# A reordering of place 0's rest in a recurrence and mixture-of-experts kernel, with four more sums in exact parts

## The chip, the cores and the metric

The kernel runs on one core of a Trainium2 chip. The metric is device time in microseconds, as a median over runs. A core has five engines with queues of their own: TensorE (PE in the profile; its weight loads are shown as PEld), VectorE (DVE), ScalarE (ACT), GpSimd (POOL) and SyncE (SP), which here only issues transfers. TensorE writes to PSUM, 8 banks of 2 KB per partition; the other data lie in SBUF.

## The reference

A gated linear attention over 4 batches, 8 heads, 768 steps and a head size of 48, whose output rows (3072 of 384 numbers) go to a mixture of 8 experts, of which each row visits one.

```
for t in range(S):
    state = alpha[:, :, t, :, None] * state + np.einsum('bhd,bhe->bhde', k[:, :, t], v[:, :, t])
    y[:, :, t] = np.einsum('bhd,bhde->bhe', q[:, :, t], state)
x = y.transpose(0, 2, 1, 3).reshape(B * S, H * D)
logits = x @ w_gate
expert_idx = np.argmax(logits, axis=1)
gate_w = softmax(logits)[np.arange(N), expert_idx]
for e in range(E):
    rows = expert_idx == e
    out[rows] = gate_w[rows, None] * (np.maximum(x[rows] @ w1[e], 0.0) @ w2[e])
```

## The kernel before

**Attention.** The 768 steps are cut into 6 chunks of 128. With 4 batches that makes 24 units `s`; `s // 4` is the chunk, `s % 4` the batch. The loop `for i in range(-4, NT)` is a software pipeline written out by hand: iteration ("step") `i` does the scores of unit `i`, the transposes of unit `i + 1`, the operands of unit `i + 2`, the logits and stored rows of unit `i - 2`, and the running sums of the logarithms of alpha of a unit ahead. The order in which the code calls these functions is the order of each engine's queue (`manual_schedule`); only the waits between engines are found automatically.

- `load` (L388) puts the transfers of alpha, k, q and v on SP. `singly` and `loads_for` set which units are loaded in which step, one at a time at first, then in pairs.
- `logs` (L396) takes the logarithm of alpha on ACT. `cums` (L413) turns it into running sums by one float32 matmul of 128 x 384 and takes `exp` of it with both signs on ACT (L419, L420). For units from `APART` = 11 on, the logarithm is split: ACT writes a float16 part `hi` (L401), DVE the remainder `lo` (L406), and two matmuls (L415, L416) add up the two parts. `sums_to` says how many units' sums are done by step `i`: units 4 and 5 in step 1, 6 and 7 in step 2, 8 in step 3, and so on. The second sum of steps 0 to 2 comes after `attend`.
- `operands` (L462) multiplies k and q by these exponentials on POOL. `transposes` (L472) turns them on PE; DVE or ACT copies the result (L476, L478). `scores` (L485), `mask` (DVE, L493), `read_state` (L512), `attend` (L522), `keys_values` (L533) and `rows` (L559) are PE's work in a step.
- `scale_state` (L500, POOL) decays a unit's state. In the first unit of a chunk it needs `decay_cols` of that step (PE L453, DVE L455). In step 4 it stands ahead of the operands on POOL; in steps 8, 12, 16 and 20 behind them.

**Routing and early rows.** From step 5 on, DVE and POOL count, rank and place the rows by expert. The experts' "places" are processed one after another, largest capacity first. In step 21 the first 256 rows of place 0 (`EARLY`) are gathered (`early_gather`). In step 23 `early_turn` transposes them (L647) ahead of the masks, and `early_layer1` (L654) computes their hidden layer while the last units are routed.

**Place 0's rest.** After the attention, the 168 remaining rows of place 0 are computed. The order is: the gather of them (L822, POOL); layer 2 of early block 0 in two halves (`early_layer2`, L1181) and its scatter (L1046 on ACT, L1050 on POOL); the gather of place 1; the first half of early block 1; `turn` (PE L832, copies L833) of the rest; the second half of early block 1 and its scatter; `rest_layer1` (L1193), whose eight hidden tiles f0 to f7 are evicted in turn by ACT (even ones, L1201) and DVE (odd ones, L1198). Behind each odd one DVE does a piece of `places()` (L1125 to L1169), the bookkeeping for rows that do not fit. Then come the weights and the gather of place 2, POOL's copies of it (L842) for SP's transposing transfers (L843), DVE's weight sums for place 1, and `rest_layer2`: three sums of eight matmuls (L1209) with a copy each (L1212), between which `turn` of place 1 and DVE's `row_sums` are called.

**Places 1 to 7** use a scheme with seven products in place of eight (L938, L1003, L1020), which needs the sums of weights (L193, L196) and of rows that DVE prepares.

Of the kernel before, what the change touches and what calls it, by code (L numbers as in the profile page):

```python
# [8 lines left out]
F32 = mybir.dt.float32  # L9
# [11 lines left out]
def kernel(  # L21
# [43 lines left out]
    HC = C // 2  # L65


    APART, HS = 11, 512.0
    assert NB * C == S and FB * C == F and DB * C == Dm and D <= DP


# [1 line left out]
    SR = NJ * C  # L73
    CAP0, STEP = 424, 8
    caps = [CAP0 - STEP * i for i in range(E)]
    EARLY = 256
    CG = 2
    NG = NB // CG
    TG = CG * B
# [292 lines left out]
    with tc.tile_pool(name="ld", bufs=6) as ld, \  # L372
# [11 lines left out]
        def load(s, n, many):  # L384
# [6 lines left out]
            for i in range(many):  # L391
                st[s + i][n] = t[:, i]

        def logs(s):
            t = work.tile([C, Dm], F32, name="lna", bufs=4)
            nc.scalar.activation(t[:], st[s]["a"].rearrange("s h d -> s (h d)"), AF.Ln)  # L396
            st[s]["lna"] = t
            if s >= APART:

                st[s]["hi"] = work.tile([C, Dm], F16, name="hi", bufs=2)  # L400
                nc.scalar.mul(st[s]["hi"][:], t[:], HS)  # L401
# [7 lines left out]

        def cums(s, bank="cum"):  # L410
            cum = ps.tile([C, 512], F32, name="cum", tag=bank)
            if s < APART:
                nc.tensor.matmul(cum[:, :Dm], lhsT=cum_m[:], rhs=st[s]["lna"][:], start=True, stop=True)  # L413
            else:
                nc.tensor.matmul(cum[:, :Dm], lhsT=cum_h[:], rhs=st[s]["hi"][:], start=True, stop=False)  # L415
                nc.tensor.matmul(cum[:, :Dm], lhsT=cum_r[:], rhs=st[s]["lo"][:], start=False, stop=True)  # L416
            cp = work.tile([C, Dm], F32, name="cp", bufs=6)
            icp = work.tile([C, Dm], F32, name="icp", bufs=6)
            nc.scalar.activation(icp[:], cum[:, :Dm], AF.Exp, scale=-1.0)  # L419
            nc.scalar.activation(cp[:], cum[:, :Dm], AF.Exp)  # L420
            st[s]["cp"], st[s]["icp"] = cp, icp
# [42 lines left out]
                    d[e][:].rearrange("s (a p d) -> s a p d", a=2, p=NP), op=ALU.mult,  # L464
                )

        def transposes(s):
            d = st[s]
            for i, n in enumerate(("kT", "qT")):
                tp = ps.tile([C, NP, C], F32, name="tp", bufs=2)  # L470
                for p in range(NP):
                    nc.tensor.transpose(tp[:, p, :], pair(kqb[s % 3][:, i], p), ident[:])  # L472
                d[n] = work.tile([C, NP, C], F32, name=n)

                if 0 < s < B - 1 or i and s < NT - B - 2:
                    nc.vector.tensor_copy(d[n][:], tp[:])  # L476
                else:
                    nc.scalar.copy(d[n][:], tp[:])  # L478
# [124 lines left out]

        loaded = dict(a=0, k=0, q=0, v=0)

        singly = {-5: "aakq", -4: "kqav", -3: "akq", -2: "aav", -1: "kq", 0: "avakq", 1: "vkq"}

        def load_next(n, many):
            load(loaded[n], n, many)
# [28 lines left out]
        eg["h"] = early.tile([C, FB, EARLY], F32, name="h0")  # L638
        held = {}

        def early_turn():
            t = ld.tile([C, 2, H, D], F32, name="k_sb", bufs=3)
            eg["xT"] = t.rearrange("p b h d -> p (b h d)").rearrange("p (a t) -> p a t", a=DB)
            for j in range(EARLY // C):
                tp = ps.tile([C, DB, C], F32, name="tp", bufs=2)
                for a in range(DB):
                    nc.tensor.transpose(tp[:, a, :], eg["xg"][:, j, a * C : (a + 1) * C], ident[:])  # L647
                nc.scalar.copy(eg["xT"][:, :, j * C : (j + 1) * C], tp[:])

        def early_layer1(f):  # L650
            hp = ps.tile([C, NP, C], F32, name="tp", bufs=2) if f % 3 else ps.tile([C, NP, C], F32, name="sB")
# [44 lines left out]
        for i in range(-4, NT):  # L696
            loads_for(i)
            do(scores, i)
            if i < NT - 1:
                do(result, i - 1)  # L700
            do(logits, i - 2)
            if i >= B:
                do(add_state, i - 1)
            do(gate, i - 2)
            if i > 0:
                for s in new_logs(i):
                    logs(s)
            if i == NT - 1:
                early_turn()
            if 0 < i < NT and i % B == 0:  # L710
                decay_cols(i // B)
            do(mask, i, 0)
            do(mask, i, 1)
            if i < B:
                do(add_state, i - 1)
            do(transposes, i + 1)
            sums = list(new_sums(i))
            for s in sums[:1]:
                cums(s)
            if i < 0:  # L720
                for s in sums[1:]:
                    cums(s, "x")
            do(gate_weight, i - 2)
            route(i)
            for s in new_logs(i):
                if s >= APART:
                    low_part(s)
            do(keep_rows, i - 2)
            if len(sums) == 1:
                decay_out(sums[0])  # L730
            if i == -1:
                for s in range(2):
                    decay_out(s)

            if B - 1 <= i < 2 * B - 1:
                decay_out(i + 1, (1,))
            if i == NT - 2:
                si = next(se)[1]
                eg["si"] = lambda j, r: si[:r, j : j + 1]
            if i == B:  # L740
                scale_state(i)
            do(operands, i + 2)
            if i > B and i % B == 0:
                scale_state(i)
            if 0 < i + 1 < NT and (i + 1) % B == 0:
                decay_rows((i + 1) // B)
            elif i >= 0:
                do(scale_state, i + 1)
            one_hots(nc.gpsimd, *on_gpsimd.get(i, ()))
            do(read_state, i)  # L750
            do(attend, i)
            if i == NT - 2:
                result(i)
            if i >= 0 and sums[1:]:
                cums(sums[1])
                for s in sums:
                    decay_out(s, (0,) if i else (0, 1))
            do(keys_values, i)
            if i == NT - 3:
                held["tok"] = ps.tile([C, NC], F32, name="tok", tag="cum")  # L760
                tokens(held["tok"][:], *range((NG - 1) * TG))
                se = early_gather()
            do(rows, i - 1)
            if i in counts_in:
                counts(counts_in[i], counted(i - 1))
            if i < 0:
                for s in new_sums(i + 1):
                    logs(s)
            if i == -3:
                second_consts()  # L770
            if i in (-4, 0, 1):
                for j in {-4: (0, 1, 2), 0: (3,), 1: (4,)}[i]:
                    late_consts(j)
            if 12 <= i < 22:
                fetch_part(groups[0], i - 12)
# [397 lines left out]
    def cols_of(t, c0):  # L1173
        return lambda j, r: t[:r, c0 + j : c0 + j + 1]

    def early_layer2(j, part):

        if part == 0:
            eg["z"] = mps.tile([C, 512], F32, name="pA", tag="pA")
        for f in range(part * FH, (part + 1) * FH):  # L1180
            nc.tensor.matmul(  # L1181
                eg["z"][:, :Dm], lhsT=eg["h"][:, f, j * C : (j + 1) * C], rhs=groups[0]["w2"][:, f, :],
                start=(f == 0), stop=(f == FB - 1),
            )

    def rest_layer1(g, beside):
        n = g["n"]
# [27 lines left out]
    g0["gi"], g0["si"] = cols_of(g_e, EARLY // C), cols_of(s_e, EARLY // C)  # L1215

    gather(g0)
    early_layer2(0, 0)
    pl = places()
    early_layer2(0, 1)  # L1220
    scatter(eg, 0, C, eg["z"][:, :Dm])
    gp, sp = next(pl)
    for i, g in enumerate(groups[1:], 1):
        g["gi"], g["si"] = cols_of(gp, i * NJ), cols_of(sp, i * NJ)
    gather(groups[1])
    early_layer2(1, 0)
    for _ in turn(g0):
        pass
    early_layer2(1, 1)
    scatter(eg, 1, C, eg["z"][:, :Dm])  # L1230
    def beside(i):

        work = [z_halves(groups[i - 1])]
# [6 lines left out]
    for i, g in enumerate(groups):  # L1240
# [17 lines left out]
            layer1(g, beside(i), begin, last)  # L1258
        else:
            rest_layer1(g, pl)  # L1260
        if i == 0:
            weights(1, 2)
        weights(i + 2, 1)
        if i + 2 < E:
# [10 lines left out]

        def turned():
            if i == 0:
                yield from turn(nxt)
                row_sums(nxt)
                return  # L1280
            z_whole(groups[i - 1], nc.scalar.copy, 0, 1)
            yield
            if nxt:
                row_sums(nxt)
            z_whole(groups[i - 1], nc.scalar.copy, 2)
            z_whole(groups[i - 1], nc.vector.tensor_copy, 3)
            yield
            if i + 2 < E:
                for _ in x_halves(groups[i + 2]):
                    pass  # L1290
            yield
# [5 lines left out]
        if last:  # L1297
            for _ in between:
                pass
            for j, r in blocks(g):  # L1300
                rows_layer2(g, j, (*([] if j == 0 else ready), FH - 1, FB - 1))
                scatter(g, j, r, g["z"][:r, :Dm], shared=j == NJ - 2)
        elif i:
            rest[0](lambda: ahead(*((1,) if i == E - 2 else (1, 2))), between)
        else:
            ahead(1)
            rest_layer2(g, 0)
            next(between)
            rest_layer2(g, 1)
            next(between, None)  # L1310
            rest_layer2(g, 2)
        weights(i + 2, 2)
    in_order.close()
# [51 lines left out]
```

## Time and profile before

| what | value |
|---|---|
| median of 8 runs | 402.53 us (400.36 to 407.0) |
| the profiled execution's own time | 400.35 us |
| its span, first to last instruction | 398.6 us |
| mean granted TensorE clock | 0.995 |
| PE, PEld, DVE, ACT, POOL busy | 96, 82, 53, 56, 37% |
| HBM read, written | 49.00 MB, 9.58 MB |
| attention: first scores to last | 9.2 to 132 us |
| place 0's rest: first L1181 to first L938 | 148.3 to 181.2 us |

Times in the trace are microseconds from the span's start. A line of the timeline gives start, duration, engine, source line, operation, output and inputs, shape and count, and in brackets the idle time before it with what ended it. A float32 matmul appears as two records. Busy times of PE are no proof that it runs at its peak, since matmul ends are modelled; the distance between the starts of two groups is a better measure.

### The profile page before, as it was taken

The numbers are of one execution on the slowest core, as the hardware profiler recorded it, in microseconds if no ns is written. First come the engines' busy times: TensorE is split into PE (matmuls) and PEld (weight loads), VectorE is DVE, ScalarE is ACT, GpSimd is POOL, SyncE is SP. The second block draws the span as 40 slices with busy tenths as digits, with TensorE's granted clock in tenths as the row PEclk, the third lists the DMA queues.
The fourth block names the chain that finished last, engine by engine and source line by source line (L and its number), as shares of the span: only waits on it lengthen the run. The fifth ranks groups of instructions, "written<-read, shape, count | busy, mean of one in ns | idle before, by whom it ended". The sixth has DMA issues, their size and how long they took to land.

```text
span 398.6 us, 9107 instructions
## 1 busy us (share of the span) xinstructions
PE 384.4 (96%) x3390; PEld 327.3 (82%) x3390; DVE 212.9 (53%) x651; ACT 224.9 (56%) x515; POOL 148.5 (37%) x203
## 2 busy tenths in 40 slices
PE   7999999999999999879999999999999999999994
PEld 4678888888888875869979979979979979979852
DVE  5554656776666574374771682582483483561200
ACT  5575767777655430114466766765765766763640
POOL 6547464599587004850023016007007003011041
PEclk9999999999999999989999999999999999999999
DMA  9999998999964118689247768667866965611311
GB/s 172 193 215 225 203 228 182 227 207 243 242 189 139 64 41 296 216 228 215 42 181 175 163 184 186 197 199 168 213 197 158 218 197 130 188 23 53 59 57 55
DMA packets 153905, 67.44 MB, mean 169 GB/s; under 512 B 136699, under 2 KB 148082, under 8 KB 153860
## 3 DMA queue, kind: packets, MB, share of 16 engines
q1 hardware_dynamic: 148756, 57.13, 59.8%
q0 software_dynamic: 3408, 9.64, 8.0%
q8 instruction: 27, 0.44, 0.5%
q10 hardware_dynamic: 1696, 0.08, 0.3%
q14 instruction: 18, 0.15, 0.1%
HBM read 49.00 MB, written 9.58 MB: 147 GB/s over the span
## 4 chain that ended last, share of the span: by engine, by line
PE 66%; issue 22%; POOL 4%; DVE 2%; ACT 2%; DMA 2%; POOLq 0%; ACTq 0%; DVEq 0%
PE pA L938 7%; PE pC L1020 5%; PE sA L485 5%; PE tp L472 5%; PE y L522 5%; PE pB L938 5%; PE pA L1003 4%; PE x L559 4%; PE pA L1181 3%; PE y L512 3%; POOL out_dram L1050 3%; PE pC L938 2%; PE pB L1003 2%; PE tp L654 2%; PE cum L413 2%
## 5 line engine op out<-in xcount | busy, mean ns | idle before, releaser
L1050 POOL DMA_INDIRECT out_dram<-zo,sp x25 | 26.0, 1039 | 137.5 <-ACT zo L1075 127.4
L193 DVE TENSOR_TENSOR h_sb<-pB,u 128x208 f32<-128x208 f32 (+6 forms) x56 | 20.1, 359 | 53.5 <-PE pB L938 39.6
L462 POOL TENSOR_TENSOR kqb<-k_sb,icp 128x384 f32<-128x384 f32 x23 | 22.9, 998 | 31.4 <-PE y L533 18.1
L1020 PE MATMUL pC<-h_sb,w 128*128 128x416 f32 (+5 forms) x96 | 33.9, 496 | 0.0
L880 ACT COPY u<-pA 128x208 f32<-128x208 f32 (+6 forms) x68 | 21.2, 311 | 18.5 <-PE pA L1003 11.5
L938 PE MATMUL pA<-t,s 128*128 128x208 f32 (+6 forms) x112 | 28.6, 337 | 0.8
L485 PE MATMUL sA<-qT,kT 48*128 48x128 f32 x192 | 27.7, 284 | 0.9 <-DVE qT L476 0.9
L485 PE MATMUL sB<-qT,kT 48*128 48x128 f32 x192 | 27.7, 285 | 0.0
L938 PE MATMUL pA<-xgT,w 128*128 128x208 f32 (+6 forms) x112 | 27.7, 329 | 0.0
L822 POOL DMA_INDIRECT xg<-x_rows,gp x25 | 24.2, 967 | 7.0 <-issue 6.8
L472 PE MATMUL tp<-ident,kqb 128*128 128x128 f32 x192 | 26.2, 279 | 0.6 <-DVE kqb L462 0.6
L1020 PEld LDWEIGHTS pC<-h_sb,w 128*128 128x128 f32 x96 | 18.0, 190 | 10.3 <-issue 3.7
L485 PEld LDWEIGHTS sA<-qT,kT 48*128 48x128 f32 x192 | 23.1, 187 | 3.8 <-ACT kT L478 1.1
L949 ACT ACTIVATE h_sb<-h_sb 128x208 f32<-128x208 f32 (+6 forms) x28 | 10.3, 366 | 25.2 <-DVE h_sb L193 22.0
L938 PE MATMUL pB<-t,w 128*128 128x208 f32 (+6 forms) x112 | 23.8, 335 | 0.0
L462 POOL TENSOR_TENSOR kqb<-q_sb,cp 128x384 f32<-128x384 f32 x23 | 23.0, 1001 | 1.8 <-DMA q_sb<-in_q_dram 1.5
L541 ACT COPY yT<-y 128x512 f32<-128x512 f32 x24 | 14.0, 585 | 16.8 <-PE y L533 9.4
L472 PEld LDWEIGHTS tp<-ident,kqb 128*128 128x128 f32 x192 | 20.5, 140 | 3.4 <-issue 1.2
L938 PE MATMUL pC<-xgT,w 128*128 128x208 f32 (+6 forms) x112 | 23.1, 329 | 0.0
L485 PEld LDWEIGHTS sB<-qT,kT 48*128 48x128 f32 x192 | 23.1, 187 | 0.0
L493 DVE TENSOR_TENSOR dA<-sA,cmask 128x512 f32<-128x512 f32 x24 | 16.5, 688 | 10.7 <-PE sB L485 10.5
L938 PEld LDWEIGHTS pA<-t,s 128*128 128x128 f32 x112 | 19.1, 189 | 3.3 <-ACT u L880 2.0
(264 smaller groups left out, 991.0 us busy)
## 6 DMA issues: line engine op xcount, KB each, us to landing
w<-in_moe_w_dram SPq DMA_DIRECT2D x14, 1536.0 KB
x_rows<-xs SPq DMA_DIRECT2D x24, 192.0 KB
v_sb<-in_v_dram SPq DMA_DIRECT2D x10, 384.0 KB
k_sb<-in_k_dram SPq DMA_DIRECT2D x9, 384.0 KB
q_sb<-in_q_dram SPq DMA_DIRECT2D x9, 384.0 KB
a_sb<-in_alpha_dram SPq DMA_DIRECT2D x8, 384.0 KB
a_sb<-in_alpha_dram SPq DMA_DIRECT2D x8, 192.0 KB
w<-in_moe_w_dram SPq DMA_DIRECT2D x6, 256.0 KB
```

Of the source, the lines that this page charges most:

```text
L193: eng.tensor_tensor(out, a, b, op=ALU.add)
L462: eng.tensor_tensor(by_half(kq[:, i]), d[n].rearrange("s (a p) d -> s a p d", a=2), d[e][:].rearrange("s (a p d) -> s a p d", a=2, p=NP), ...
L472: nc.tensor.transpose(tp[:, p, :], pair(kqb[s % 3][:, i], p), ident[:])
L485: nc.tensor.matmul(t[:, p, :], lhsT=d["kT"][r : r + D, p, :], rhs=d["qT"][r : r + D, p, :], start=True, stop=True,)
L493: nc.vector.tensor_tensor(t[:], d["sc"][i][:], cmask[:, None, :].to_broadcast([C, NP, C]), op=ALU.mult)
L522: nc.tensor.matmul(yv(g)[o : o + D, j, :], lhsT=d["v"][:, g * NP + p, :], rhs=d["d" + "AB"[g]][:, p, :], start=(s < B and j == 0), stop=Tr ...
L822: nc.gpsimd.indirect_dma_start(out=g["xg"][:r, j, :], out_offset=None, in_=x_d[:, :], in_offset=bass.IndirectOffsetOnAxis(ap=g["gi"](j, r) ...
L880: nc.scalar.copy(t[:, :m], bank["A"][:, :m])
L938: nc.tensor.matmul(out, lhsT=ops[n_][0], rhs=ops[n_][1], start=first and n_ == names[0], stop=True, skip_group_check=True,)
L1003: nc.tensor.matmul(out, lhsT=lhs, rhs=rhs, start=first and f == 0, stop=True, skip_group_check=True)
L1020: nc.tensor.matmul(d2[:, :n], lhsT=w2[:, f, 2 * C :], rhs=h[:, f, :n], start=(f == 0), stop=(f == FB - 1),)
L1050: ins = nc.gpsimd.indirect_dma_start(out=out[:, :], out_offset=bass.IndirectOffsetOnAxis(ap=g["si"](j, r), axis=0), in_=zo[:r], in_offset= ...
```

## The change

It has five edits.

1. Sums in exact parts start at unit 9 instead of 11, and units 5 and 7 have them too. The `lo` of 5 and 7 is made on DVE inside `transposes`, between the copies of kT and qT.
2. Alpha 8 and 9 are loaded one at a time, alpha 8 ahead of v, k and q in step 1.
3. In step 8, as in step 4, `scale_state` stands ahead of the operands.
4. `early_turn` is split: block 0 is turned behind `read_state` of the last step, block 1 behind its `attend`.
5. Place 0's rest: the second half of early block 1 goes behind `rest_layer1`, in a PSUM buffer of the transposes (`tp`); its scatter goes with it, and so on POOL ahead of the gather of place 2. All of place 1's `turn` goes ahead of the weight sums and of the first `rest_layer2`, whose 24 matmuls follow one another; `row_sums` comes behind the first of the three.

`EARLY` is written as `2 * C`, which is 256 as before.

```diff
-    APART, HS = 11, 512.0
+    APART, HS = 9, 512.0
...
+        def apart(s):
+
+            return s >= APART or s in (5, 7)
...
-            if s >= APART:
+            if apart(s):
...
-            if s < APART:
+            if not apart(s):
...
-        def transposes(s):
+        def transposes(s, *lows):
             d = st[s]
             for i, n in enumerate(("kT", "qT")):
+                if i:
+                    for t in lows:
+                        low_part(t)
...
-        singly = {-5: "aakq", -4: "kqav", -3: "akq", -2: "aav", -1: "kq", 0: "avakq", 1: "vkq"}
+        singly = {-5: "aakq", -4: "kqav", -3: "akq", -2: "aav", -1: "kq", 0: "avakq", 1: "avkq", 2: "a"}
...
-            if i == NT - 1:
-                early_turn()
...
-            do(transposes, i + 1)
+            do(transposes, i + 1, *[s for s in new_sums(i) if apart(s) and s < APART])
...
-            if i == B:
+            if i in (B, 2 * B):
                 scale_state(i)
             do(operands, i + 2)
-            if i > B and i % B == 0:
+            if i > 2 * B and i % B == 0:
                 scale_state(i)
...
             do(read_state, i)
+            if i == NT - 1:
+                early_turn(0)
             do(attend, i)
+            if i == NT - 1:
+                early_turn(1)
...
-    def early_layer2(j, part):
-
-        if part == 0:
-            eg["z"] = mps.tile([C, 512], F32, name="pA", tag="pA")
-        for f in range(part * FH, (part + 1) * FH):
+    def early_layer2(j, fs):
+
+        if 0 in fs:
+            t = "tp" if j else "pA"
+            eg["z"] = mps.tile([C, DB, C], F32, name=t, tag=t).rearrange("p a c -> p (a c)")
+        for f in fs:
...
+        if FB - 1 in fs:
+            scatter(eg, j, C, eg["z"][:, :Dm])
...
-    early_layer2(1, 0)
+    early_layer2(1, range(FH))
     for _ in turn(g0):
         pass
-    early_layer2(1, 1)
-    scatter(eg, 1, C, eg["z"][:, :Dm])
+
...
             rest_layer1(g, pl)
-        if i == 0:
+
+            early_layer2(1, range(FH, FB))
             weights(1, 2)
...
             if i == 0:
-                yield from turn(nxt)
+                for _ in turn(nxt):
+                    pass
+                yield
                 row_sums(nxt)
-                return
+                yield
...
         else:
+            next(between)
             ahead(1)
             rest_layer2(g, 0)
             next(between)
             rest_layer2(g, 1)
-            next(between, None)
             rest_layer2(g, 2)
```

More of the change, by code (lines that the diff above doesn't have):

```diff
@@ L75 @@
     caps = [CAP0 - STEP * i for i in range(E)]
-    EARLY = 256
+    EARLY = 2 * C
     CG = 2
@@ L639, with early_turn @@
         held = {}
[L641 to L648, printed above, removed]
+        def early_turn(j):
+            if j == 0:
+                t = ld.tile([C, 2, H, D], F32, name="k_sb", bufs=3)
+                eg["xT"] = t.rearrange("p b h d -> p (b h d)").rearrange("p (a t) -> p a t", a=DB)
+            tp = ps.tile([C, DB, C], F32, name="tp", bufs=2)
+            for a in range(DB):
+                nc.tensor.transpose(tp[:, a, :], eg["xg"][:, j, a * C : (a + 1) * C], ident[:])
+            nc.scalar.copy(eg["xT"][:, :, j * C : (j + 1) * C], tp[:])
         def early_layer1(f):
@@ L1217 @@
     gather(g0)
-    early_layer2(0, 0)
+    early_layer2(0, range(FH))
     pl = places()
-    early_layer2(0, 1)
-    scatter(eg, 0, C, eg["z"][:, :Dm])
+    early_layer2(0, range(FH, FB))
     gp, sp = next(pl)
```

## The prediction

> **What bounds the kernel now.** I read the page first. PE is busy 96% of a span of 398.6 us; DVE, ACT and POOL are at 53, 56 and 37%.
>
> ```profile
> PE 384.4 (96%) x3390; PEld 327.3 (82%) x3390; DVE 212.9 (53%) x651; ACT 224.9 (56%) x515; POOL 148.5 (37%) x203
> ...
> PE   7999999999999999879999999999999999999994
> ```
>
> The matmul ends are modelled, so a 9 is no proof of a full engine. The proof for the attention is the rhythm in PE's timeline: steps are 5.13 us apart again and again (steps 7, 9, 11, 14 to 16), and steps with a float32 sum 5.44. PE alone sets that pace. The digits 8 and 7 in slices 17 and 18 are place 0's rest, so I read that stretch next, microsecond by microsecond (columns: window, its length, then busy time of PE, PEld, DVE, ACT, POOL, the granted clock, DMA share, GB/s).
>
> ```profile
> 167.00:168.00 1.00, 0.55 (x4) 0.43 (x4) 1.00 (x2) 0.00 (x0) 1.00 (x2) 1.00 0.36 131
> ...
> 170.00:171.00 1.00, 0.00 (x0) 0.00 (x0) 0.97 (x5) 0.00 (x0) 0.83 (x3) 1.00 0.00 0
> ...
> 174.00:175.00 1.00, 1.00 (x7) 1.00 (x6) 1.00 (x3) 0.30 (x1) 0.70 (x2) 0.50 1.04 422
> ```
>
> PE starves from 167.5 to 173.1, and from 173.2 to 176.6 it runs at half the granted clock. The chain of waits names what it starved for:
>
> ```profile
> 166.72 0.33 DVE h_sb L1198
> 167.05 2.26 DVE ve L1148
> ...
> 171.26 0.23 DVE h_sb L1198
> ...
> 172.84 0.25 DVE h_sb L1198
> ...
> 173.13 0.93 PE pA L1209 x2
> ```
>
> Layer 2 (L1209) needs all eight hidden tiles; DVE evicts the odd ones (L1198), and between them works off the bookkeeping of `places()`. Tile 5 is evicted at 171.26 and tile 7 at 172.84, though their matmuls were issued by 166.6.
>
> **Part 1: place 0's rest.** Its cost now: first L1193 matmul at 159.55, first of place 1 (L938) at 181.23: 21.7 us. Its work: 8 x 0.855 (L1193) = 6.84; three L1209 sums at the undisturbed third one's pace (178.84 to 181.23, 2.39) = 7.2; twelve transposes, 0.72 per six (178.12 to 178.84), = 1.44. That is 15.5; 6.2 us are lost, 1.7 of them (half of 3.4) to the clock.
>
> After it, PE's order is: transposes of g0, L1193, the early rows' second half, all twelve transposes of place 1, then 24 L1209 matmuls in a row.
> - *Before L1193.* The second g0 block must now reuse the buffer that DVE empties, since the early sum holds the other. Transposes 156.13 to 156.55, DVE copy (156.72 to 157.28), transposes, ACT copy 0.26: L1193 begins near 158.3 with 1.5 us of PE idle inside, against 159.55.
> - *L1193* 6.85: to 165.15. *Early second half*, 2.4 (156.86 to 159.2 before): 167.55. This covers DVE's bookkeeping: f1 evicted near 160.2, then 1.3 of bookkeeping (L1137 to L1145), f3, 2.1 (L1148 to L1162 with a scan at 0.29, as the larger scan of L267 has), f5, 1.5, f7: 166.3 with evictions at 0.33.
> - *Transposes* 1.44 plus 0.45 of waits for copies (ACT's copy of the early sum, 0.48, frees a buffer): 169.45. *L1209* 7.2 without a wait: 176.65. DVE's four weight sums (0.65 each) and five row sums (0.36 each) follow its copies at 169.5 and end at 173.9, in time.
>
> Place 1 starts 181.23 - 176.65 = **4.6 us** sooner. The places behind it are PE-paced (39.8 of 40 us in each window from 200 to 360), so it should reach the end.
>
> What moves with it: the second scatter of the early rows (L1050) sits on POOL ahead of the gathers of place 2, and is issued at 168 instead of 160.92. Four gathers (1.28 each), four copies of L842 (3.12), a memset and the gathers of place 3 all go 7 us later: copies from 174.3 to 177.4. On SP the load of place 2's w1 waits for L1193 alone and goes earlier; its transposes (9.4 us for four) wait for the copies and end near 180 to 184; w2 behind them is issued near 180 to 184 (181.70 now), wanted by DVE at 203.47 - 5 = 198. Cover: 14 us or more.
>
> **Part 2: sums in exact parts for 5, 7, 9, 10.** PE's timeline, the time from the sum to the next group:
>
> ```profile
> 33.89 0.81 PE L413 MATMUL cum<-lna,cum_m 128*128 128x384 f32 x2
> 34.63 0.66 PE L512 MATMUL y<-qT,U 48*48 48x128 f32 x16
> ```
>
> ```profile
> 44.79 0.33 PE L415 MATMUL cum<-hi,cum_h 128*128 128x384 f16 x1
> ...
> 45.21 0.66 PE L512 MATMUL y<-qT,U 48*48 48x128 f32 x16
> ```
>
> 0.74 against 0.42: 0.32 each, and the steps say the same (5.44 - 5.13). On ACT each costs a `hi` of 0.52 (L401), on DVE a `lo` of 0.56 (L406). For 9 and 10 they lie in DVE's idle stretches (29.9 to 31.6, 35.3 to 37.4). `lo` 5 (about 17.6) delays qT(2), which ends by 18.8, wanted at 20.1. `lo` 7 is the doubtful one. It comes near 22.8 to 23.1, ahead of qT(3) and the gate weight, while POOL runs its operands of step 4 from 22.41 to 24.37. One row shows what such a meeting can do:
>
> ```profile
> 139.13 0.29 DVE L267 TENSOR_TENSOR_SCAN pr<-keep,sel 128x64 f32<-128x64 f32 x1
> ...
> 166.91 3.12 POOL L842 COPY xh<-xg 128x768 uint16<-128x768 uint16 x4
> 166.97 2.33 DVE L1148 TENSOR_TENSOR_SCAN ve<-nb,zero_e 128x8 f32<-128x8 f32 x1
> ```
>
> A scan of an eighth the size took 2.33 instead of 0.29 and ended as POOL's third copy did. No `lo` row overlaps a POOL operand, so I bound: free, `lo` 7 ends by 23.6 and the sum gains 0.32; held to 24.37, it ends at 24.95, and PE, there at 24.3, loses 0.6 less 0.32, so 0.3. I take 0, the middle. The sum: 3 x 0.32 + 0 = 0.96.
>
> The Trainium skill, "SBUF — State Buffer", "Practical consequences", says that a DVE instruction with two SBUF inputs contends with a GpSimd instruction that reads SBUF, and the second to issue blocks fully. That speaks against this change: by it `lo` 7 is held (0.3 lost instead of 0), and DVE's sums in part 1 are held wherever POOL's later copies meet them. The scan row agrees with it; no row here shows it for `lo`.
>
> **Part 3: step 8 decays its state first.** The step takes 5.75 where 12 and 16 take 5.47, and shows why:
>
> ```profile
> 56.10 0.65 PE L512 MATMUL y<-qT,U 48*48 48x128 f32 x16 [0.20 <-POOL U L500]
> ```
>
> U(8) ran at 55.54, behind the operands (53.62, 54.57). First, it runs when E is there (54.74), done by 55.3: 0.28 saved. The operands move from 53.6 to 55.3 and end at 57.3, wanted at 59.87; `lo` 11 may then wait for them until 57.3, wanted at 60.8. Nothing else pays.
>
> **Part 4, at nothing.** Alpha 8 goes ahead of v3, k5, q5 on SP (192 KB, some 0.9 us at the 215 GB/s of that stretch); k5 is used at 25.76 with 7 us to its transposes, v3 at 29.07. Cover gone only if loads slip by 4 us. It is needed, since `hi` 9 now wants alpha 9 a step earlier. Early rows turned behind the state: same six transposes, only later in PE's order; the gather landed by 131.3, the transposes ran at 132.02, and now run at 132.6 and 134. Bounds: -0.3 to +0.3. EARLY stays 256.
>
> **Sum.** 4.6 + 0.96 + 0.28 = 5.8 us. Against the profiled execution (400.35, span 398.6 and 1.75 around it): 394.5. That execution is the fastest of those shown; their median is 402.53, 2.2 above, so I forecast 402.5 - 5.8 = **396.7** for the median.
>
> **Rivals.**
> - *The releases from PE come late again.* ACT evicted tile 2 at 164.57 and tile 4 at 168.88, DVE tile 3 at 166.72, all 2.3 to 4.9 us after their matmuls' modelled ends, with nothing else to wait for. The trace does not say why. If that recurs, 1.2 us earlier, f7 is evicted near 169.8, the transposes' copies end at 171.3, L1209 runs to 178.2: 3.0 instead of 4.6, total 4.2, **398.3**. For it: it is in the only trace. Against: it falls in the time of POOL's gathers (162.25 to 166.9), which move away.
> - *It hardly does what it should.* On top of that DVE's nine sums begin at 171.4, meet POOL's four copies (174.3 to 177.4) and are held 3 us, to about 179; gain 1.5 to 2, and `lo` 7 loses 0.3: total near 2, **400.6**.
> - *Slower.* One mechanism: SP's queue. Place 2's w2 sits behind four transposes that wait for POOL's late copies, and DVE's weight sums wait in order for w2, with the row sums of place 2 behind them. It begins to cost when w2 lands after 198, a microsecond for each; it must land after 204 to undo all. With 8 us of landing (1.5 MB at 190 GB/s) w2 would have to be issued after 196, 12 us beyond my latest estimate. At 206: **404.5**.
>
> **Chances.** Forecast 0.47, late releases 0.28, hardly 0.15, slower 0.10. A measurement of this kernel tells 0.5%, 2.0 us, from no change: forecast and late releases are faster, hardly is the same, the last is slower: 0.75, 0.15, 0.10. The range takes in the sum against the fastest execution (394.5, and 0.9 below it for a free `lo` 7, 0.32, and a scan and waits that vanish) and the hardly case: 393.6 to 400.8.
>
> **What would show it.** Right: the window 167 to 173 with PE full and no half clock behind it; L1209 as one block of 24; first L938 4 to 6 us earlier relative to the first L1181; sums of 5, 7, 9, 10 at 0.42; step 8 at 5.47. Wrong: L1198's last eviction still the releaser of PE; DVE's `lo` 7 or weight sums longer than 0.7; a wait for w2's DMA in place 1.

## The result, and the profile after

The changed kernel takes 399.16 us (median of 23 runs, 397.58 to 402.8) against 402.25 for the kernel before (65 runs beside it): a ratio of 0.9925 [0.9907, 0.9943], so 3.0 us are saved. The forecast was 5.8 saved. The profiled execution is one of its longer ones: 401.43 us with a span of 399.7, where before's was one of its shortest, so the two spans must not be subtracted. I compare stretches of the traces. In the code after, L1191 is `early_layer2`, L1205 `rest_layer1` (evictions: L1210 on DVE, L1213 on ACT), L1221 `rest_layer2`, L841 and L842 `turn`, L851 POOL's copies, L947 place 1's first layer, L420 the matmul of `lo`, L410 `lo` itself.

The page: PE is as busy as before, and the weak slices have moved from the middle to the front.

```profile
PE 384.3 (96%) x3390; PEld 326.9 (82%) x3390; DVE 215.8 (54%) x655; ACT 226.6 (57%) x519; POOL 149.8 (37%) x203
...
PE   7987999999999999899999999999999999999994
```

**Place 0's rest, the gain.** The three windows that starved or ran at half clock, after (same columns as before):

```profile
167.00:168.00 1.00, 1.00 (x9) 1.00 (x9) 0.97 (x6) 0.31 (x1) 0.00 (x0) 1.00 0.82 282
170.00:171.00 1.00, 1.00 (x4) 0.57 (x3) 0.34 (x2) 0.00 (x0) 0.00 (x0) 1.00 0.00 0
174.00:175.00 1.00, 0.86 (x8) 0.68 (x7) 0.82 (x2) 0.46 (x2) 0.69 (x2) 1.00 1.00 410
```

PE is busy 0.86 to 1.00 of them and the clock is 1.00. DVE's and PE's timelines say why:

```profile
166.59 0.33 DVE L1210 TENSOR_SCALAR h_sb<-pC 128x168 f32<-128x168 f32 x1 [0.29 <-PE pC L1205]
166.84 0.17 DVE L1157 TENSOR_TENSOR_SCAN ve<-nb,zero_e 128x8 f32<-128x8 f32 x1
```

```profile
169.81 2.74 PE L1191 MATMUL tp<-w,h 128*128 128x384 f32 x8
...
174.57 7.11 PE L1221 MATMUL pA<-h_sb,w 128*128 128x168 f32 x48
181.52 0.51 PE L947 MATMUL pA<-xgT,w 128*128 128x208 f32 x2
```

Tile 3 is evicted at 166.59, as soon as its matmuls are through, and the scan takes 0.17 us, not 2.33. Layer 2 is one block of 24 matmuls (48 records). From the first layer-2 matmul of the early rows to place 1 it is now 153.10 to 181.52, **28.42 us instead of 32.94: 4.5 less.**

**The early steps, the loss.** The first layer-2 matmul itself comes at 153.10, not 148.29. From first scores to last, attention takes 126.4 us in this execution, 121.8 before. Of the difference, 2.6 us are step 3, 7.87 long (5.26 before); step 2 is 1.0 longer and steps 4 to 6 together 1.5. In step 3 before, ACT and PE hardly wait:

```profile
27.65 0.52 ACT L396 ACTIVATE lna<-a_sb 128x384 f32<-128x384 f32 x1 [0.26 <-DMA a_sb<-in_alpha_dram]
30.67 0.94 PE L559 MATMUL x<-iw,yT 128*64 128x104 f32 x16 [0.16 <-ACT xs L584]
```

ACT's timeline in it after:

```profile
30.40 0.52 ACT L400 ACTIVATE lna<-a_sb 128x384 f32<-128x384 f32 x1 [2.10 <-DMA a_sb<-in_alpha_dram]
30.95 0.52 ACT L405 ACTIVATE hi<-lna 128x384 f16<-128x384 f32 x1
...
32.60 0.59 ACT L591 ACTIVATE xs<-x,gw 128x384 f32<-128x384 f32 x1
```

and PE's:

```profile
33.25 1.66 PE L566 MATMUL x<-iw,yT 128*64 128x104 f32 x16 [2.05 <-ACT xs L591]
```

ACT stands for 2.1 us because alpha 9 has not landed. SP issued it at 25.06, behind alpha 8 (21.50) and the transfers of v, k and q; it is used at 30.40, 5.3 us later. In SP's timeline it is the first of these two:

```profile
25.06 2.13 SPq L388 DMA_DIRECT2D a_sb<-in_alpha_dram  x2
```

Behind alpha 9's logarithm in ACT's queue are `hi`, a transpose copy, both exponentials and the stored rows (xs), for which PE stands 2.05 us. Then the granted clock falls to 0.50 (windows 34 to 36), and the rows' matmuls take 1.66 us instead of 0.94.

### The profile page after: what moved, and what is told of

Its sections match the earlier page's. It is cut to its first block, busy times and chain, and to the rows that moved or that the text cites. A ratio compares the mean times of both kernels' runs of the same rounds, so it can differ in the third digit from the quotient of the medians.

```text
span 399.7 us, 9118 instructions
## 1 busy us (share of the span) xinstructions
PE 384.3 (96%) x3390; PEld 326.9 (82%) x3390; DVE 215.8 (54%) x655; ACT 226.6 (57%) x519; POOL 149.8 (37%) x203
## 4 chain that ended last, share of the span: by engine, by line
PE 64%; issue 22%; POOL 5%; DMA 3%; ACT 3%; DVE 2%; POOLq 0%; ACTq 0%; DVEq 0%
PE pA L947 7%; PE pC L1029 5%; PE pA L1012 5%; PE pB L947 5%; PE sA L492 5%; PE tp L479 5%; PE y L529 5%; PE x L566 3%; POOL out_dram L1059 3%; PE y L519 2%; PE pB L1012 2%; PE pC L947 2%; PE pA L1221 2%; PE tp L661 2%; DMA dec<-icp 2%
## 5 line engine op out<-in xcount | busy, mean ns | idle before, releaser
L947 PE MATMUL pA<-t,s 128*128 128x208 f32 (+6 forms) x112 | 28.7, 338 | 0.8
L492 PE MATMUL sA<-qT,kT 48*128 48x128 f32 x192 | 28.6, 291 | 0.9 <-DVE qT L483 0.9
L492 PE MATMUL sB<-qT,kT 48*128 48x128 f32 x192 | 28.6, 291 | 0.0
L947 PE MATMUL pA<-xgT,w 128*128 128x208 f32 (+6 forms) x112 | 27.7, 329 | 0.0
L492 PEld LDWEIGHTS sA<-qT,kT 48*128 48x128 f32 x192 | 23.9, 193 | 3.9 <-ACT kT L485 1.1
L566 PE MATMUL x<-iw,yT 128*64 128x104 f32 x368 | 21.6, 261 | 3.3 <-ACT xs L591 3.3
L492 PEld LDWEIGHTS sB<-qT,kT 48*128 48x128 f32 x192 | 23.9, 193 | 0.0
L947 PE MATMUL pB<-t,w 128*128 128x208 f32 (+6 forms) x112 | 23.8, 335 | 0.0
L947 PE MATMUL pC<-xgT,w 128*128 128x208 f32 (+6 forms) x112 | 23.1, 329 | 0.0
L947 PEld LDWEIGHTS pA<-t,s 128*128 128x128 f32 x112 | 19.0, 189 | 3.7 <-ACT u L889 2.1
```

The lines of the kernel that those rows point to most:

```text
L492: nc.tensor.matmul(t[:, p, :], lhsT=d["kT"][r : r + D, p, :], rhs=d["qT"][r : r + D, p, :], start=True, stop=True,)
L566: nc.tensor.matmul(d["x"][o : o + HC, m, : D2 + E], lhsT=d["yT"][:, m // 2, m % 2, o : o + HC], rhs=iw[:, m, :], start=True, stop=True,)
L947: nc.tensor.matmul(out, lhsT=ops[n_][0], rhs=ops[n_][1], start=first and n_ == names[0], stop=True, skip_group_check=True,)
```

## The experiments

Times below are medians. Runs 1 to 4 were made on one chip (before: 402.01 us there), 5 to 8 on a second (402.33), 9 to 12 on a third, where before took only 396.60; so kernels are compared on one chip. "Rest" is the stretch from the first L1191 matmul to the first of place 1, "attention" first scores to last, each in that kernel's profiled execution.

| run | us (n) | ratio to before | rest | attention |
|---|---|---|---|---|
| 1 rest only | 398.09 (6) | 0.9909 [0.9880, 0.9938] | 28.42 | 127.0 |
| 2 no sums | 397.21 (5) | 0.9895 [0.9871, 0.9920] | 28.43 | 122.0 |
| 3 from 9 only | 400.12 (12) | 0.9962 [0.9930, 0.9995] | 28.43 | 124.0 |
| 4 5 and 7 only | 397.37 (5) | 0.9888 [0.9863, 0.9913] | 28.42 | 121.1 |
| 5 no rest | 404.03 (12) | 1.0042 [1.0022, 1.0062] | 33.73 | 127.3 |
| 6 alpha in pairs | 398.96 (11) | 0.9925 [0.9903, 0.9946] | 28.43 | 126.8 |
| 7 log 9 later | 398.67 (6) | 0.9929 [0.9902, 0.9956] | 28.42 | 122.9 |
| 8 alpha 9 sooner | 397.99 (6) | 0.9910 [0.9886, 0.9934] | 28.43 | 122.3 |
| 9 gather first | 396.44 (12) | 0.9992 [0.9961, 1.0023] | 28.43 | 123.0 |
| 10 half behind | 397.18 (12) | 1.0008 [0.9983, 1.0033] | 27.61 | 122.0 |
| 11 turn ahead | 398.62 (12) | 1.0028 [0.9995, 1.0060] | 29.48 | 122.8 |
| 12 ten, not nine | 396.42 (12) | 0.9987 [0.9958, 1.0016] | 28.42 | 122.1 |

### 1 and 5: which part of the change pays

Run 1 is the kernel before with edit 5 alone; run 5 is the changed kernel with edit 5 undone.

```diff
 # 1: edits 1 to 4 undone
-    APART, HS = 9, 512.0
+    APART, HS = 11, 512.0
-            return s >= APART or s in (5, 7)
+            return s >= APART
-            if i in (B, 2 * B):
+            if i == B:
```
```diff
 # 5: edit 5 undone
-            early_layer2(1, range(FH, FB))
...
+    early_layer2(1, 1)
+    scatter(eg, 1, C, eg["z"][:, :Dm])
```

> The kernel before with edit 5 alone (place 0's rest reordered); sums, alpha loads, step 8 and the early turn as before. Theory A (the edit of place 0's rest is worth what the profile of the changed kernel shows between the first matmul of early layer 2 and the first of place 1, 32.9 to 28.4 us, and the attention edits lose 1 to 2 us of it): 4.5 us faster than before, near 397.7, so faster than the changed kernel by about 1.5. Theory B (the attention edits gain 1.2 and the reordering is worth only 1.8 because the places behind it give the rest back): 1.8 faster, near 400.4.

> The kernel before with edits 1 to 4 and without the reordering of place 0's rest. Theory A (the reordering gives 4.5 and the four other edits lose about 1.4): 1 to 1.5 us slower than before, near 403.2, with ACT waiting 1.5 to 3 us for alpha 9 in step 3. Theory B (the attention edits gain 1.2): near 400.8. On the way: place 0's rest lasts 32.9 us again, with releases of tiles 2 to 4 some 2 to 5 us behind their matmuls' modelled ends, if these belong to the old order; near 30 without them if they were an accident of the one trace.

Edit 5 alone saves 3.9 us; without it the rest of the change costs 1.7. The two add up to about what the whole change does (2.2 against 3.0, with intervals of over a microsecond each). The rest takes 28.42 in run 1 and 33.73 in run 5. (Run 1's attention of 127.0 is not typical of that kernel: in its profiled execution, 403.18 us, ACT waited 2.78 us for alpha 8.) In run 5's chain of waits the old picture is back:

```profile
172.46 0.33 DVE h_sb L1207
172.80 2.22 DVE ve L1157
...
178.55 0.26 DVE h_sb L1207
178.80 0.04 issue
178.85 0.93 PE pA L1218 x2
```

Tile 3 again comes 3.6 us after its matmuls, the scan again takes 2.2 us beside POOL's copies, and PE waits for the last eviction until 178.85.

### 2, 3 and 4: which of the sums lose

All three start from the changed kernel.

```diff
 # 2: no further sums in exact parts
-    APART, HS = 9, 512.0
+    APART, HS = 11, 512.0
-            return s >= APART or s in (5, 7)
+            return s >= APART
 # 3: from 9 on, not 5 and 7
-            return s >= APART or s in (5, 7)
+            return s >= APART
 # 4: 5 and 7, else from 11 on
-    APART, HS = 9, 512.0
+    APART, HS = 11, 512.0
```

> The changed kernel without its four new sums in exact parts (they start at unit 11 again); alpha 8 and 9 are still loaded one by one and sooner. Theory A (the new parts cost more than their 0.32 us each give, by waits for alpha 9 and by DVE's low parts held behind POOL): 1.5 us faster than the changed kernel, near 397.6, no wait of ACT for alpha of over 1 us in step 3. Theory B (the parts gain 0.96): 1 us slower than the changed kernel, near 400.1.

> The changed kernel with exact parts from unit 9, but not for 5 and 7. Theory A1 (the price is alpha 9, wanted in step 3: in the profile of the changed kernel ACT waits 2.1 us for it, and with it the copy of kT, the exponentials and the rows behind it): within 0.4 us of the changed kernel, and the wait for alpha in step 3 still there. Theory A2 (the price is unit 7, whose low part took 1.24 us on DVE and held qT, the gate weight and ACT's rows): faster than the changed kernel by 1 us or more. Theory B: slower by 0.3 to 0.6.

> The changed kernel with exact parts for 5, 7 and from 11 on, but not for 9 and 10. Theory A1 (alpha 9 in step 3 is the price): 1 us or more faster than the changed kernel. Theory A2 (unit 7's low part is the price): within 0.4 us of it. Theory B: slower by 0.6.

Without 9 and 10 (runs 2 and 4) the kernel is 1.8 to 2.0 us faster than the changed one (1.2 to 1.5 by the ratios); 5 and 7 make no difference that can be told (397.21 and 397.37). With 9 and 10 alone it is 2.9 slower than without. So the loss is in 9 and 10. Run 3's trace has the wait of the changed kernel: ACT 1.71 us for alpha 9, PE then 1.85 for xs. In runs 2 and 4 neither is there, and run 4 shows a granted clock of 1.0. Runs 2 and 4 are the fastest on that chip and can't be told apart.

### 6, 7 and 8: is it alpha 9's arrival?

These start from the changed kernel too.

```diff
 # 6: alpha 8 and 9 in a pair again
-... 1: "avkq", 2: "a"}
+... 1: "vkq"}
 # 7: unit 9's logarithm a step later
-    APART, HS = 9, 512.0
+    APART, HS = 10, 512.0
-            return s >= APART or s in (5, 7)
+            return s >= APART or s in (5, 7, 9)
 # 8: alpha 9 loaded right behind alpha 8 in step 1
-... 1: "avkq", 2: "a"}
+... 1: "aavkq"}
```

> The changed kernel with alpha 8 and 9 loaded as before, in one pair behind v3, k5 and q5. Theory A1 (alpha 9 in step 3 is the price, and it lands later as part of a pair issued after those): slower than the changed kernel by 0.5 to 1.5 us, near 400.2, with the wait of ACT for alpha in step 3 of 2.5 us or more. Rival (the alpha loads are hidden in any order): within 0.3 us of the changed kernel.

> The changed kernel with the logarithm and the float16 part of unit 9 made in step 4, where the sum needs them, not in step 3; the same four sums in exact parts (9 handled as 5 and 7 are, the general scheme starts at 10). Theory A1 (ACT's in-order wait for alpha 9 in step 3 is the price): 1.8 to 2.8 us faster than the changed kernel, near 396.9, and no wait of ACT for alpha over 1 us in step 3. Rival (the parts of 9 and 10 cost by DVE's low parts held behind POOL): within 0.5 us of the changed kernel.

> The changed kernel with alpha 9 loaded in step 1 ahead of v3, k5 and q5, right behind alpha 8. Theory A1: the wait for alpha 9 in step 3 shrinks from 2.1 us to under 0.5, 1.5 to 2.5 us faster than the changed kernel, near 397.2. Rival (the transfer engines are full in this stretch, and what alpha 9 gains k5 and q5 lose on POOL): within 0.5 us of the changed kernel, with POOL waiting longer for k5 or q5.

In run 8 the wait for alpha 9 is gone, step 3 takes 5.19, and the time is 1.2 us below the changed kernel's (0.6 by the two ratios, whose intervals overlap). In run 6 nothing changes: loaded as a pair, alpha is late too (2.70 us). So alpha 9's lateness is probably a large part of the loss, at 0.6 to 1.2 of its 1.5 to 1.8 us; the traces show the wait and its end, but the times alone would not settle it. The loading edit in the change does not cure it. Run 7 removes the same wait and recovers 0.5 by the medians and nothing by the ratios: unit 9's remainder then comes late for PE, as its timeline shows.

```profile
35.15 0.44 PE L420 MATMUL cum<-lo,cum_r 128*128 128x384 f32 x1 [0.74 <-DVE lo L410]
```

### 9: do the gathers make the evictions late?

In the old order POOL gathers place 2 while tiles 2 to 5 are due. Run 9, made from run 4 as all that follow, puts that back into the new order.

```diff
             rest_layer1(g, pl)
-            early_layer2(1, range(FH, FB))
             weights(1, 2)
         weights(i + 2, 1)
         if i + 2 < E:
             gather(groups[i + 2])
+        if i == 0:
+            early_layer2(1, range(FH, FB))
```

> Base: the version with 5 and 7 in exact parts and from 11 on (397.4 us), whose place 0's rest takes 28.42 us. Only the order on POOL and SP differs: place 2's weights and its four gathers go ahead of the second half of early block 1, so the gathers run beside the evictions of place 0's hidden tiles, as in the old order; PE's, ACT's and DVE's orders stay. Theory G (the late evictions of the old order come from POOL's gathers beside them): the evictions of tiles 2 to 4 come 1 to 4 us late again, but the early half covers 2.4 us of it; the rest takes 29 to 31 us, the time is 398 to 400. Theory P (they come from the order of PE's own work, not from the gathers): evictions 0.85 us apart, the rest 28.4, the time 397.4 or a little less, since place 2's copies on POOL come earlier.

The traces look as theory P says: the gathers run from 162.57 to 167.19, beside the evictions, and tile 3 is evicted without delay.

```profile
163.43 0.33 DVE L1210 TENSOR_SCALAR h_sb<-pC 128x168 f32<-128x168 f32 x1 [0.28 <-PE pC L1205]
163.68 0.16 DVE L1157 TENSOR_TENSOR_SCAN ve<-nb,zero_e 128x8 f32<-128x8 f32 x1
```

But the chip had changed, and so had the kernel before (396.60). Run 11 below has the old order of PE's work and shows no late eviction on this chip either, so run 9 can't decide between the two theories: what it shows is that gathers do not delay the evictions on the third chip.

### 10 and 11: which half of edit 5

```diff
 # 10: early half stays behind, place 1 turned between the sums as before
-                for _ in turn(nxt):
-                    pass
-                yield
+                yield from turn(nxt)
                 row_sums(nxt)
 # 11: early half back ahead of rest_layer1, place 1 turned before the 24 matmuls
             rest_layer1(g, pl)
-            early_layer2(1, range(FH, FB))
```

> Base as in the run before (397.4). Only half of the reordering: the second half of early block 1 stays behind the hidden layer of place 0's rest, but place 1's rows are again turned between the three layer-2 sums, with DVE's weight sums ahead of them. If the cover for DVE's bookkeeping is what pays (theory C): evictions on time, DVE's weight sums (4 x 0.69) ahead of its copy of the turned rows hold the second six transposes about 1 us; the rest takes 28.5 to 29.5 us, the time is 397.5 to 398.5. If the turning pays as much as the cover (theory T): 30 to 31 us, 399 to 400.

> Base as in the runs before (397.4). Only the other half: the second half of early block 1 is back ahead of the hidden layer, its scatter and the gathers of place 2 too, but all of place 1's rows are turned before the 24 matmuls of layer 2. Theory C: the late evictions and the scan held behind POOL's copies come back, only the transposes (1.5 us) cover some of it; the rest takes 31.5 to 33 us, the time is 400.5 to 402. Theory T: 30 to 31 us, 399 to 400.

Run 10 is 0.7 us slower than run 9 and run 12, run 11 2.2 slower. So the cover for DVE's bookkeeping is the half that counts, as theory C has it, but its price for run 11 was too high, because a part of the old picture is missing: up to tile 7 run 11 has the old order on every engine, and yet **its evictions are on time** on this chip (tile 3 at 164.56, 0.86 after tile 2). What is left is a meeting of DVE and POOL. DVE's timeline, then POOL's:

```profile
164.56 0.33 DVE L1210 TENSOR_SCALAR h_sb<-pC 128x168 f32<-128x168 f32 x1 [0.28 <-PE pC L1205]
...
167.82 2.85 DVE L1178 SCALAR_TENSOR_TENSOR xx<-xx,kx 128x24 f32<-128x24 f32 x1
170.60 0.32 DVE L1210 TENSOR_SCALAR h_sb<-pB 128x168 f32<-128x168 f32 x1
```

```profile
168.28 3.29 POOL L851 COPY xh<-xg 128x768 uint16<-128x768 uint16 x4
```

A bookkeeping instruction of 24 elements takes 2.85 us instead of 0.18, and the last eviction and the copy of the turned rows wait behind it; PE stands 2.85. The rest is 1.06 longer by it than run 12's. That is half of the 2.2; the other half is not shown by one trace, but most of run 11's executions have a mean granted clock of 0.996 or less, against two of run 12's twelve, so a half clock behind this stall is likely in it. Run 10 has the shortest rest of all (27.61) and loses it at once: DVE's row sums come last, the first of them beside POOL's copies (3.11 us, in run 12 0.41 ahead of them), PE waits 1.03 for them in place 1, and that place takes 33.20 instead of 31.67.

### 12: ten, not nine

```diff
-    APART, HS = 11, 512.0
+    APART, HS = 10, 512.0
```

> Base as in the runs before (397.4). One more sum in exact parts, unit 10, but not 9, whose logarithm then needs its alpha a step later than in the changed kernel. If the loss of the early steps is alpha 9's alone (theory A): no wait of ACT for alpha in step 3, the sum of 10 saves 0.3, 397.1. If it is ACT's and DVE's load by the added parts (theory B): PE waits for the remainder of 10 or for ACT's copies behind its scaling in steps 4 and 5, 397.7 to 398.2.

ACT does not wait for alpha in step 3, as theory A has it, and the step with the sum of 10 takes 5.23, 0.2 less than before's 5.44. The next takes 6.15 against 5.14: PE waits 0.47 for xs among others. That is theory B's sign. Run 4 was not made on this chip, so the total can't weigh the two.

## Why the prediction was right, and where not

**Place 0's rest: 4.6 forecast, 4.5 measured.** Its working holds nearly line by line, counted from the first layer-2 matmul: L1205 begins after 9.8 us (10.0 forecast), layer 2 after 21.5 (21.2), place 1 after 28.42 (28.36). DVE's sums end at 178.9 and POOL's copies begin at 179.37, so they do not meet. No wait for w2 shows in place 1: the slower rival did not come about.

What the working took as given, late releases by PE in the old order (the signals that a tile's matmuls are done), seems to be the larger part of the matter, and it isn't the same on every chip. On the first two chips all 39 runs of before beside experiments 1 to 8 have a mean granted clock of 0.996 or less; the half clock behind the old stall, half of 3.4 us in 398.6, makes 0.9957 by itself. On the third, 28 of 35 runs of before show 0.997 or more, and their median is 396.60. There, versions with edit 5 (runs 9 and 12) are level with before. I take it that the old order's stall is absent there, since run 11 shows its evictions on time; a trace of before on that chip was not taken, so this is argued, not shown. By the same token the 3.0 us hold for chips on which the old order stalls. The changed kernel itself was not run on the third.

**"So it should reach the end": not all of it.** Place 1 takes 31.66 us before and 32.46 after (32.32 to 32.50 in runs 1 to 4 and 6 to 8, but 31.67 in runs 9 and 12 on the third chip), since one release by PE comes a microsecond late there. DVE's timeline, after and in run 12:

```profile
189.07 0.38 DVE L193 TENSOR_TENSOR h_sb<-pB,u 128x208 f32<-128x208 f32 x1 [2.42 <-PE pA L947]
```

```profile
183.65 0.38 DVE L193 TENSOR_TENSOR h_sb<-pB,u 128x208 f32<-128x208 f32 x1 [1.42 <-PE pB L947]
```

The pB matmuls begin at 187.17 and 182.75, the same 0.87 us of work; the release comes 1.9 and 0.9 us later. That is 0.8 of the 4.5 given back. Places 2 to 7 are as before.

**The sums: +0.96 forecast, about -1.6 measured.** This is the step that failed. The matmuls did get cheaper (sum 9 to the next group 0.43, sum 10 0.44). But "for 9 and 10 they lie in DVE's idle stretches" looked at DVE alone. The bound was in part 4: "Cover gone only if loads slip by 4 us. It is needed, since `hi` 9 now wants alpha 9 a step earlier". I put that at nothing without looking for when alpha 9 lands: 30.4, where ACT wants it at 28.3. And I did not name what stands behind it in ACT's queue. Priced by that queue, the wait is 2.05 us of PE and then up to half of 3.4 us at half clock; in the medians the parts of 9 and 10 cost 1.8 us (399.16 against 397.37; by the ratios 1.5) instead of gaining 0.64.

**`lo` 7, "I take 0, the middle".** Both ends occur, and who starts first decides. All engines' timeline, after and in run 4:

```profile
23.16 0.99 POOL L466 TENSOR_TENSOR kqb<-k_sb,icp 128x384 f32<-128x384 f32 x1 [3.11 <-DMA k_sb<-in_k_dram]
...
23.33 1.24 DVE L410 SCALAR_TENSOR_TENSOR lo<-hi,lna 128x384 fp32r<-128x384 f16 x1 [0.49 <-ACT hi L405]
```

```profile
22.58 0.55 DVE L410 SCALAR_TENSOR_TENSOR lo<-hi,lna 128x384 fp32r<-128x384 f16 x1
22.62 1.37 POOL L466 TENSOR_TENSOR kqb<-k_sb,icp 128x384 f32<-128x384 f32 x1 [2.24 <-ACT hi L405]
```

With POOL first `lo` takes 1.24; with DVE first, by 0.04 us, `lo` is free and POOL's product takes 1.37 instead of 0.99. In all ten traces with a `lo` 7 (after, runs 4 to 12) the one that starts first is not held. Step 2 takes 5.61 in run 4 and 5.68 in run 12 (`lo` 0.55 and 0.56; 5.87 before), so the free end pays 0.2 to 0.3, as bounded. In runs 5, 8 and 10 `lo` takes 0.94, 1.32 and 1.09 and the step 6.00, 6.38 and 6.14: 0.1 to 0.5 lost, where the bound was 0.3, since the gate weight and xs stand behind `lo`. The rest of the loss is a term that the working did not have: `hi` 7 can be late. `lo` waits 0.26 to 0.49 for it after and in runs 9 and 11, and the step takes 6.67 to 6.87; in runs 6 and 7 `lo` waits 0.48 and 0.68 for it, is then free (0.56), and the step still takes 6.19 and 6.37. In four of these five ACT had waited for alpha 7 (0.19 to 0.56).

The Trainium skill, "SBUF — State Buffer", "Who interferes with whom", says among its practical consequences that the order of issue decides which of the two blocks. The pair of rows above agrees with that, and its warning about two SBUF inputs was the right one to weigh. Run 11's row agrees less plainly: there DVE's instruction starts at 167.82 and POOL's copies at 168.28, while POOL's last gather runs from 167.41, and yet it is DVE that takes 2.85.

**Step 8: 0.28 forecast, 0.28 measured where it comes.** The step takes 5.47 after and in runs 3, 4, 6, 7 and 12. In runs 2, 5 and 8 to 11, which have the edit too, it takes 5.81 to 6.50, no better than 5.75: there the wait is one stage back. PE's timeline of run 10:

```profile
54.73 0.41 PE L457 MATMUL ep<-ident,er 4*128 4x4 f32 x4 [0.29 <-POOL er L446]
```

POOL's `er`, which waits for the decays by DMA, is then the last to come. I had named what follows U on POOL, not what comes ahead of it.

**Early rows turned later: nothing forecast, 0.24 lost.** From the last scores to the first L1191 it takes 17.60 us after and in runs 2 to 5 (17.36 before), inside the bounds given.

**The total.** 4.5 - 0.8 (place 1) - 1.6 (sums of 9 and 10) + 0 (5 and 7) + 0.3 (step 8) - 0.2 (early rows) is 2.2; measured 3.0, with an interval of 2.3 to 3.7. So half of the forecast saving came. The 399.16 lies close to the 398.3 of the rival with late releases, but that is mostly chance: place 0's rest had none after the change, place 1 had one, and the sums, not the releases, took the larger part.

One reading of the prediction was wrong without effect: step 16, listed among those of 5.13 us, takes 5.47 before, as its own part 3 says; the 5.13 hold for steps 7, 9, 11 and 13 to 15.

## What to carry to other kernels

When an operation moves to an earlier step, look up in the trace when its input lands and write down what stands behind it on its in-order engine; a saving of 0.3 us in PE turned into 2 us of PE's waiting for a copy that had nothing to do with the moved sum. Independent PE work put behind a group whose results others must evict can cover what makes those evictions late, even when its cause isn't known. Small DVE instructions need the same care as large ones wherever POOL copies run: here one of 24 elements cost 2.85 us.

## What the runs showed of the hardware

- **Late releases.** In the old order evictions came 0.9 to 4.9 us after their matmuls' modelled ends (traces of before and of run 5), in the new order none did in place 0's rest, but one of 1.0 us in place 1 (after, runs 1 to 4 and 6 to 8). On the third chip neither order showed them (runs 9, 11, 12), and there gathers beside the evictions did not cause them (runs 9 and 11). The cause stays open; a trace of before on the third chip would be the next thing to take.
- **A rival for them, untested.** The updates of semaphores (the counters by which one engine signals another) that stand in a trace number 5502 to 5592 in before, after and runs 1 to 8, and 6153 to 6158 in runs 9 to 12, for 9107 to 9118 instructions. Before's trace has no update by PE between 159.72 and 164.55, though two evictions ran in that time, then one at 164.55, 166.69 and 168.86, each just ahead of a late eviction, and from there several 0.07 apart; after's has them 0.86 or 1.71 apart in the same work. So it could be the recording of the profile that holds PE's signals up on those chips. No run here tests it.
- **DVE against POOL.** Beside POOL's copies or products a scan of 8 elements took 2.33 us instead of 0.17, a product of 24 elements 2.85 instead of 0.18, a row sum 3.11 instead of 0.41, `lo` up to 1.32 instead of 0.55.
- **The clock.** About 2 us in which PE stood (31.2 to 33.25, after) were followed by a clock of 0.50 for 3.4 us (33.3 to 36.7 by the shares of its windows). In run 5, 1.94 us (to 32.18) were followed by 6.8 us at 0.50 (33.7 to 40.5). In run 3, 1.85 us, and in run 11, 2.85 us, were followed by none; run 11's 24 matmuls behind took 6.95 us, the undisturbed pace. So a stall of this length cost its own length and 0, 1.7 or 3.4 us more, and the runs here do not say which beforehand.
- **Chips differ.** The same kernel before took 402.0, 402.3 and 396.6 us on three chips, a spread nearly twice the change's effect.
